# An attention and channel-mix kernel: third and fourth head pair prepared as one tile, five fillers for eight, the last output turned by a DMA, and a new table of order

## The chip, the cores and the metric

The kernel runs on one core of a Trainium2 chip. A core has TensorE (PE: matrix multiplications, its weight loads are shown apart as PEld), VectorE (DVE), ScalarE (ACT), GpSimd (POOL) and SyncE (SP, which here only issues DMAs). Each engine takes its instructions in the order in which they were written, and waits for others by semaphores. The metric is the device time of one execution in microseconds (us), as the median of several runs; one further execution was profiled.

## The reference, cut to what matters

```python
# q, k, v: (4, 8, 768, 64) float32; proj: (64, 6)
q_bits = (q @ proj > 0);  k_bits = (k @ proj > 0)          # 6 bits per token
mask   = q_bucket[..., :, None] == k_bucket[..., None, :]  # bucket = the 6 bits as a number
scores = where(mask, (q @ k.T) / sqrt(64), -1e9)
attn   = softmax(scores);  o = attn @ v
x      = o with heads side by side                          # (4, 768, 512)
x_prev = x one token earlier, 0 for the first
xk = mu_k * x + (1 - mu_k) * x_prev;  xr likewise with mu_r
kk = max(xk @ w_k, 0);  vv = kk * kk @ w_v
out = sigmoid(xr @ w_r) * vv                                # (4, 768, 512) float32
```

It is a hash-masked attention over 4 batches of 8 heads, followed by a channel mix (below: the mix) with weights w_k (512 x 1024), w_v (1024 x 512) and w_r (512 x 512).

## The kernel before, in words

**Pairs.** The 32 heads are worked in 16 pairs, numbered 0 to 15, four pairs to a batch. A pair goes through these steps, each of them an operation of a plan (`add`), with the name that this text uses:

- load: `ldq` brings q and k (float32) into the tile `nat`, `ldv` brings v into `vn`, all issued on SP (L330, L335).
- prepare: q and k are split into two half-precision parts in the tile `nh`: `hi` (L398, DVE) is the rounded value, `lo` (L401, DVE) the rest. Then `tr` (L405, a DMA transpose issued on SP) turns `nh` into the tile `a`, with the head's 64 rows of `hi` over 64 rows of `lo`. For pairs 0 and 1 (`add_prep_turn`, L446) all of this is done by PE transposes (L478, L512) with evacuations on ACT and DVE, since DMAs are slow to arrive at the start; there `hi` is L467, the bits come out of PE as L489 and go into `nh` by L497 (`ex`), and the turned tile is evacuated by L517 (`evt`).
- bits (`bits`, L427, PE): the six projections of q and k, in 16 small matmuls; `bx` (L431, DVE) makes signs of them; four `row` copies (L443, POOL) write the sign rows of q and k of both heads into the tile `a`, so that the product of q and k also tells whether the buckets agree.
- scores (`sc`, L544, PE): 9 steps of 1024 columns per pair, each into a PSUM tile of two banks; `exp` (L548, ACT) takes each step to the tile `pt`. A step needs the sign rows of the heads and halves that its columns touch.
- `oo` (L571, PE): the weighted sum of v, three groups of 12 matmuls for each of the two heads; `rc` (L582, L584, L585) and `ob` (L589) normalise it on DVE. For pairs 0 to 3 a thirteenth matmul (L566) adds a small constant.
- turn: the 128 columns of the pair are turned for the mix, either by six PE transposes (`ot`, L599) and a DVE copy (`xt`, L602), or by a DMA transpose on SP (`otd`, L605). Which pairs go by PE is the tuple `OT_PE` (L40).
- mix inputs: DVE makes the shifted difference and `xk`, `xr` (L612, L630 to L644).

After the fourth pair of a batch its mix follows (`add_moe`, L648): `kp` (L659, PE) with relu on ACT (L663) and squares on DVE (L666), `r` (L679, PE) with a tanh on ACT (L682), `v` (L692, PE), the product `os` on DVE (L699) and the store `st` on SP (L702). The weights of the mix are loaded by `wl` (SP) and cast by `wc` (L304, POOL).

**Order.** The operations are not emitted as they are added. `Plan.schedule` (L123) puts them out in the order of a table, `ORDER` (L17), whose numbers are the places at which the operations were added, and gives each PSUM user a bank from a second table, `BANKS` (L72). So each engine's sequence is fixed by hand, and an instruction that is not ready holds up all that stand behind it on its engine. A PSUM bank that is taken again adds a wait for the operation that read it last.

**Whole or in halves.** `MERGED` (L37) lists the pairs whose q and k are prepared together (`add_prep`, L390): one `hi`, one `lo` over 24 blocks and one transposing DMA. Pairs 2 and 3 are not in it: they have a `hi`, a `lo` and a `tr` for q and another for k, 12 blocks each. `nh` has two buffers, `nat` three, so that `hi` of a pair waits for the transpose of the pair two earlier, and a load for `lo` of the pair three earlier.

**Fillers.** PE starts with 14 matmuls on zeros (L246) and has 8 fillers of two such matmuls each (L251), strewn by `ORDER` among the first steps of the work.

Of the kernel before, what the change touches and what calls it, by code (L numbers as in the profile page):

```python
# [128 lines left out]
def kernel(  # L129
# [34 lines left out]
    MERGED = tuple(range(4, 16))  # L164
    FIRSTS = (0, 1)
    JOINT = ()
    OT_PE = (0, 1, 2, 3, 15)
# [611 lines left out]
```

## Time and profile before

| what | us |
|---|---|
| median of 3 runs (lowest and highest) | 243.16 (242.25 to 243.25) |
| the profiled execution's own time | 242.0 |
| span in that profile, first to last instruction | 240.2 |
| PE busy | 234.1 (97%) |
| ACT busy | 181.9 (76%) |
| DVE busy | 179.8 (75%) |
| POOL busy | 99.7 (41%) |
| granted TensorE clock | 1.00 throughout |

How to read it: the profiled execution ran 1.2 us under the median, and its own time is 1.8 us over its span. Busy shares are averages over stages that differ: attention of the first pairs alone, attention and mix side by side, and the last mix alone. In rows of the timeline, what stands ahead is the start and the duration of a merged piece in us from the start of the span; a merged piece's duration reaches to the end of its last instruction, and neighbours on a pipelined engine overlap by some hundredths.

### The profile page before, as it was taken

The page shows a single profiled execution, that of the slowest core. Times are in us where ns is not written, and L with a number is a line of the kernel's source. Part 1 is how long each engine was busy: PE and PEld are TensorE (multiplying, and loading weights), DVE is VectorE, ACT ScalarE, POOL GpSimd, SP SyncE. Part 2 cuts the span into 40 slices and gives each one's busy share as a digit, 9 for nine tenths or more (in the row PEclk, how much of TensorE's full clock was granted, in tenths as well). Part 3 has the DMA queues.
Part 4 walks back from the last instruction along what each step waited for, and adds up shares of the span by engine and source line. Part 5 has one row for each costly group of instructions (what it writes and reads, how often), then busy time and mean ns, then how long its engine had stood idle before and what let it go on. Part 6 is the DMA issues. An engine that isn't in the chain of part 4 may idle for free.

```text
span 240.2 us, 6251 instructions
## 1 busy us (share of the span) xinstructions
PE 234.1 (97%) x2515; PEld 147.8 (62%) x2532; DVE 179.8 (75%) x388; ACT 181.9 (76%) x242; POOL 99.7 (41%) x148
## 2 busy tenths in 40 slices
PE   8999999999999999999999999999999999999994
PEld 6985776776766565656456656665566564455442
DVE  3488789999998898989868896887167867348232
ACT  2699999999999999889779999677884640256320
POOL 4064979989934899438087302550000000000000
PEclk9999999999999999999999999999999999999999
DMA  6989999999999999988999989401500401210333
GB/s 225 304 222 274 232 242 260 279 197 362 279 253 284 273 213 294 249 302 206 276 163 241 249 177 234 136 0 26 173 0 3 120 3 44 87 46 1 131 135 131
DMA packets 72605, 44.00 MB, mean 183 GB/s; under 512 B 54912, under 2 KB 67584, under 8 KB 72576
## 3 DMA queue, kind: packets, MB, share of 16 engines
q1 hardware_dynamic: 72208, 43.20, 70.9%
q8 instruction: 20, 0.33, 0.6%
q10 hardware_dynamic: 368, 0.39, 0.5%
q14 instruction: 9, 0.07, 0.1%
HBM read 24.12 MB, written 6.29 MB: 127 GB/s over the span
## 4 chain that ended last, share of the span: by engine, by line
PE 92%; ACT 5%; issue 1%; DVE 0%
PE ps_all L544 25%; PE ps_all L692 17%; PE ps_all L659 16%; PE ps_all L571 14%; PE ps_all L679 8%; ACT pt L548 4%; PE ps_all L427 4%; PE ps_all L489 2%; PE ps_all L512 1%; PE ps_all L478 1%; ACT kr L663 1%; PE ps_all L251 1%; PE ps_all L246 1%; PE ps_all L599 1%; PE ps_all L566 1%
## 5 line engine op out<-in xcount | busy, mean ns | idle before, releaser
L548 ACT ACTIVATE pt<-ps_all 128x1024 bf16<-128x1024 f32 x144 | 138.4, 1041 | 10.9 <-PE ps_all L544 10.3
L544 PE MATMUL ps_all<-a 128*128 128x256 f16 (+1 forms) x384 | 79.2, 325 | 0.5 <-ACT pt L548 0.3
L443 POOL COPY a<-bx 6x384 f32<-6x384 f32 x56 | 38.9, 695 | 34.4 <-DVE bx L431 19.6
L544 PEld LDWEIGHTS <-a 128*128 128x128 f16 x384 | 34.0, 98 | 23.5 <-issue 4.6
L659 PE MATMUL ps_all<-xk,wk 128*128 128x384 bf16 x256 | 48.3, 326 | 0.1
L571 PEld LDWEIGHTS <-pt 128*128 128x128 bf16 x1152 | 42.5, 97 | 8.0 <-issue 0.5
L692 PE MATMUL ps_all<-wv,k 128*128 128x512 bf16 (+2 forms) x199 | 45.6, 362 | 0.5
L571 PE MATMUL ps_all<-va,pt 128*128 128x65 bf16 x1152 | 44.8, 193 | 0.0
L663 ACT ACTIVATE kr<-ps_all 128x384 bf16<-128x384 f32 x64 | 29.4, 491 | 16.0 <-PE ps_all L659 14.4
L659 PEld LDWEIGHTS <-wk 128*128 128x128 bf16 x256 | 24.2, 98 | 17.0 <-issue 0.6
L692 PEld LDWEIGHTS <-k 128*128 128x128 bf16 x208 | 19.3, 98 | 18.9 <-issue 0.3
L699 DVE SCALAR_TENSOR_TENSOR os<-rs,ps_all 128x512 f32<-128x512 f32 (+2 forms) x26 | 16.5, 643 | 19.0 <-PE ps_all L692 13.7
L682 ACT ACTIVATE rs<-ps_all 128x512 f32<-128x512 f32 x24 | 14.3, 602 | 20.5 <-PE ps_all L679 14.1
L666 DVE TENSOR_TENSOR k<-kr 128x384 bf16<-128x384 bf16 x64 | 23.2, 389 | 8.3 <-ACT kr L663 8.3
L401 DVE SCALAR_TENSOR_TENSOR nh<-nat,nh 128x1536 f16<-128x1536 f32 (+1 forms) x16 | 27.0, 1694 | 0.2
L679 PE MATMUL ps_all<-wr,xr 128*128 128x512 bf16 x88 | 23.2, 379 | 0.4
L356 POOL TENSOR_TENSOR vt<-vn 128x384 f32<-128x384 f32 x12 | 17.8, 1485 | 12.5 <-DMA vn<-in_v_dram 11.7
L589 DVE TENSOR_TENSOR ob<-ps_all,rc 128x384 bf16<-128x384 f32 x32 | 17.5, 553 | 1.4 <-DMA xt<-ob 0.8
L431 DVE TENSOR_SCALAR bx<-ps_all 128x768 uint16<-128x768 uint16 x14 | 13.4, 956 | 5.3 <-PE ps_all L427 4.7
L398 DVE TENSOR_SCALAR nh<-nat 128x1536 f16<-128x1536 f32 (+1 forms) x16 | 15.8, 985 | 0.3 <-PE ps_all L512 0.2
L679 PEld LDWEIGHTS <-xr 128*128 128x128 bf16 x96 | 9.0, 98 | 9.0
L380 DVE SCALAR_TENSOR_TENSOR va<-ps_all,vn 128x384 bf16<-128x384 f32 x24 | 12.7, 548 | 0.5 <-PE ps_all L375 0.2
(77 smaller groups left out, 188.9 us busy)
## 6 DMA issues: line engine op xcount, KB each, us to landing
vn<-in_v_dram SPq DMA_DIRECT2D x16, 384.0 KB, 5.1
out_dram<-os SPq DMA_DIRECT2D x23, 256.0 KB, 2.3
nat<-in_k_dram SPq DMA_DIRECT2D x15, 384.0 KB, 4.7
nat<-in_q_dram SPq DMA_DIRECT2D x15, 384.0 KB, 5.2
wst<-in_moe_w_k_dram SPq DMA_DIRECT2D x2, 512.0 KB, 7.0
wst<-in_moe_w_r_dram SPq DMA_DIRECT2D x2, 512.0 KB, 5.8
wst<-in_moe_w_v_dram SPq DMA_DIRECT2D x2, 512.0 KB, 4.4
k<-in_moe_w_k_dram SPq DMA_DIRECT2D x1, 512.0 KB, 4.4
```

Source lines behind the costliest of these rows:

```text
L356: e.tensor_tensor(out=vt[:, :, :, 0:E], in0=src[:, :, 0:3, 0:E], in1=src[:, :, 3:6, 0:E], op=ALU.add)
L401: nc.vector.scalar_tensor_tensor(out=nh[:, :, D:P], in0=nat.rearrange("p j (c d) -> p (j c) d", d=D), scalar=QS, in1=nh[:, :, 0:D], op0=AL ...
L443: nc.gpsimd.tensor_copy(side_a[side][n % NAQ][D : D + NB, j, :].bitcast(FP32), bx_t[sx][32 * i : 32 * i + NB, :].bitcast(FP32))
L544: nc.tensor.matmul(ps[:, lo - s * STEP : hi - s * STEP], side_a["k"][sa][:, j, jc * P : (jc + 1) * P], side_a["q"][sa][:, j, q0 : q0 + hi ...
L548: nc.scalar.activation(out=pt_t[sp][:, s * STEP : (s + 1) * STEP], in_=ps_t[plan.slot[nm]], func=AF.Exp, bias=EBIAS, scale=ESC)
L571: nc.tensor.matmul(oo[:, ic * 65 : ic * 65 + 65], pt_t[sp][:, o : o + P], va_t[sa][:, j, jc, 0 : D + 1], start=(not uc and ic == 0 and jc ...
L589: nc.vector.tensor_tensor(out=ob_t[so][:, :, j * D : (j + 1) * D], in0=oo[:, :, 0:D], in1=rc_t[sr][:, 1, :].unsqueeze(2).to_broadcast([P, ...
L659: nc.tensor.matmul(ps[:, 0:HALF], wk_sb[:, d, fc * P : (fc + 1) * P], xk_t[mx[d]][:, h * HALF : (h + 1) * HALF], start=(d == 0), stop=(d = ...
L663: nc.scalar.activation(out=kr_t[sk], in_=sm(nm)[:, 0:HALF], func=AF.Relu, scale=0.5 ** 0.5)
L666: nc.vector.tensor_tensor(out=k2_t[s2][:, h * HALF : (h + 1) * HALF], in0=kr_t[sk], in1=kr_t[sk], op=ALU.mult)
L679: nc.tensor.matmul(sm(nr), xr_t[mx[d]][:, c * P : (c + 1) * P], wr_sb[:, d, :], start=(d == 0), stop=(d == NDC - 1))
L692: nc.tensor.matmul(sm(nv)[:, x0:x1], k2_t[(b * NFC + fc) % NK2][:, c * P : (c + 1) * P], wv_sb[:, fc, x0:x1], start=(fc == 0), stop=(fc == ...
```

## The change

Five edits come together.

1. `MERGED` takes in pairs 2 and 3: for each of them two `hi`, two `lo` and two transposing DMAs of 12 blocks become one of each of 24 blocks.
2. Eight fillers become five; the three that go are those which stood between the scores of pairs 2 and 3.
3. `OT_PE` loses pair 15: its output is turned by a DMA on SP instead of six PE transposes and a DVE copy.
4. `ORDER` has new numbers for all operations behind the head. (The head, up to the first scores, has the same sequence on PE.)
5. `BANKS` is new.

The diff, with the tables cut:

```diff
 ORDER = [
-    0, 16, 2, 3, 4, 21, 5, 6, 7, 20, 8, 9, 10, 11, 37, 41, 33, 26, 1, 29, 28, 36, 30, 32, 40, 69, 72, 71, 70, 74, 73, 25, 43, 27, 31, 79,
...
+    0, 34, 66, 69, 38, 30, 23, 31, 16, 68, 71, 1, 26, 25, 2, 33, 3, 67, 70, 4, 27, 20, 29, 37, 74, 22, 5, 109, 6, 40, 24, 28, 7, 19, 44, 8,
...
 BANKS = [
-    2, 6, 2, 0, 4, 0, 0, 0, 0, 4, 4, 0, 3, 7, 1, 5, 4, 6, 1, 4, 5, 3, 4, 5, 2, 3, 4, 5, 4, 3, 0, 1, 2, 3, 0, 0, 0, 1, 7, 6, 6, 0, 2, 2, 2,
...
+    3, 5, 2, 0, 0, 6, 7, 6, 5, 6, 5, 4, 3, 5, 2, 4, 3, 3, 0, 2, 1, 0, 3, 5, 3, 2, 3, 0, 1, 2, 0, 1, 2, 0, 2, 1, 0, 1, 3, 2, 1, 1, 1, 1, 1,
...
-    MERGED = tuple(range(4, 16))
+    MERGED = tuple(range(2, 16))
...
-    OT_PE = (0, 1, 2, 3, 15)
+    OT_PE = (0, 1, 2, 3)
...
-    for i in range(8):
+    for i in range(5):
         def filler(i=i):
```

Lines of the changed kernel are one less than those of before from the fillers on.

What the tables do to the order is read from the built programs. First, DVE from the sign step of the first pair to the sign step of the third (`nh_61` with `nat_60` is pair 2, `nh_62` with `nat_58` pair 3, `nh_61` with `nat_59` pair 4; `bx_67` is pair 2's signs). Before:

```order
L497 TENSOR_SCALAR nh_61<-ps_all 128x6x6
L398 TENSOR_SCALAR nh_61<-nat_60 128x12x64
L517 COPY a_63<-ps_all 128x768
L398 TENSOR_SCALAR nh_61<-nat_60 128x12x64
L401 SCALAR_TENSOR_TENSOR nh_61<-nat_60,nh_61 128x12x64 x2
L497 TENSOR_SCALAR nh_62<-ps_all 128x12x6
L275 TENSOR_SCALAR mur<-mur 128x4
...
L398 TENSOR_SCALAR nh_62<-nat_58 128x12x64
L401 SCALAR_TENSOR_TENSOR nh_62<-nat_58,nh_62 128x12x64
L431 TENSOR_SCALAR bx_67<-ps_all 128x768
L401 SCALAR_TENSOR_TENSOR nh_62<-nat_58,nh_62 128x12x64
```

And in the changed kernel, the same stretch:

```order
L496 TENSOR_SCALAR nh_61<-ps_all 128x6x6
L516 COPY a_63<-ps_all 128x768
L397 TENSOR_SCALAR nh_61<-nat_60 128x24x64
L400 SCALAR_TENSOR_TENSOR nh_61<-nat_60,nh_61 128x24x64
L274 TENSOR_SCALAR mur<-mur 128x4
L496 TENSOR_SCALAR nh_62<-ps_all 128x12x6
...
L397 TENSOR_SCALAR nh_62<-nat_58 128x24x64
L400 SCALAR_TENSOR_TENSOR nh_62<-nat_58,nh_62 128x24x64
L430 TENSOR_SCALAR bx_67<-ps_all 128x768
L397 TENSOR_SCALAR nh_61<-nat_59 128x24x64
L581 RECIPROCAL rc_89<-ps_all 128x6
L588 TENSOR_TENSOR ob_92<-ps_all,rc_89 128x6x64
```

The first half of pair 2's `hi` no longer stands ahead of the copy L517, `mur` has moved ahead of the sign step of pair 1 (L497 with `nh_62`), and the whole `lo` of pair 3 stands ahead of pair 2's `bx`, where only its first half stood.

Second, SP from the last early load of q to the transposes of pair 3 (`a2_65` is pair 2, `a3_66` pair 3). Before:

```order
L330 DMA nat0_58<-in_q_dram 128x2x384
L405 DMA_TRANSPOSE a2_65<-nh0_61 128x12x128 x2
L330 DMA nat1_59<-in_k_dram 128x2x384
L335 DMA vn2_71<-in_v_dram 128x2x384
L330 DMA nat1_59<-in_q_dram 128x2x384
L273 DMA muk_135<-in_moe_mu_k_dram 128x4x1
L335 DMA vn0_69<-in_v_dram 128x2x384
L405 DMA_TRANSPOSE a3_66<-nh1_62 128x12x128 x2
```

And in the changed kernel:

```order
L329 DMA nat0_58<-in_q_dram 128x2x384
L334 DMA vn2_71<-in_v_dram 128x2x384
L329 DMA nat1_59<-in_k_dram 128x2x384
L404 DMA_TRANSPOSE a2_65<-nh0_61 128x24x128
L329 DMA nat1_59<-in_q_dram 128x2x384
L272 DMA muk_135<-in_moe_mu_k_dram 128x4x1
L334 DMA vn1_70<-in_v_dram 128x2x384
L329 DMA nat2_60<-in_k_dram 128x2x384
L334 DMA vn0_69<-in_v_dram 128x2x384
L404 DMA_TRANSPOSE a3_66<-nh1_62 128x24x128
```

Two loads moved ahead of pair 2's transpose, and one load more stands between the two pairs' transposes.

Third, POOL around the sign rows of pairs 2 and 3 (the `COPY` rows into `a2_65` and `a3_66`; `vt0_72` and `vsu` are sums over v). Before:

```order
L443 COPY a2_65<-bx0_67 6x384 x4
L350 CAST va2_80<-vn2_71 128x12x64
L350 CAST va0_78<-vn0_69 128x12x64
L356 TENSOR_TENSOR vt0_72<-va2_80 128x390
L359 TENSOR_TENSOR vt0_72<-vt0_72 128x2x65
L362 TENSOR_TENSOR vsu0_75<-vt0_72 128x130
L269 MEMSET xt3_97 128x1
L269 MEMSET xt0_94 128x1
L443 COPY a3_66<-bx1_68 6x384 x4
```

And in the changed kernel:

```order
L442 COPY a2_65<-bx0_67 6x384 x2
L268 MEMSET xt0_94 128x1
L442 COPY a2_65<-bx0_67 6x384 x2
L268 MEMSET xt5_99 128x1
L355 TENSOR_TENSOR vt0_72<-va2_80 128x390
L358 TENSOR_TENSOR vt0_72<-vt0_72 128x2x65
L361 TENSOR_TENSOR vsu0_75<-vt0_72 128x130
L349 CAST va0_78<-vn0_69 128x12x64
L355 TENSOR_TENSOR vt0_72<-va0_78 128x390
L442 COPY a3_66<-bx1_68 6x384 x4
```

The cast of pair 2's v moved to before the rows of pair 2, and the first sum of pair 3's v to before the rows of pair 3. By the numbers of `ORDER`, the four rows of pair 3 come as q1, k1, q0, k0 before and as q1, q0, k1, k0 after (letter for side, digit for head).

On PE, between the bits of pair 2 and the first scores of pair 2, there stand before: sc1_7, sc1_4, sc1_5, two groups of oo0_1, two of oo0_0, sc1_0, a group of oo0_0; and after: sc1_7, oo0_1, sc1_3, oo0_1, sc1_0, oo0_0, sc1_4, oo0_0 (sc1_7 is step 7 of pair 1; oo0_1 a group of pair 0, head 1). The last steps on PE are v3_5_256, v3_5_384, v3_5_0 before, and v3_5_384, r3_5, r3_4, v3_4, v3_5_0 after (batch 3, chunk of 128 tokens, first column).

115 rows, old and new, of tables (BANKS, ORDER) are left out of this document.

## The prediction

> **What bounds the kernel now.** I read the page's busy shares and chain first, then the busy time by windows, then the timeline of the first 36 us and of the last 40. The page has the chain that ended last almost wholly on PE:
>
> ```profile
> PE 92%; ACT 5%; issue 1%; DVE 0%
> L548 ACT ACTIVATE pt<-ps_all 128x1024 bf16<-128x1024 f32 x144 | 138.4, 1041 | 10.9 <-PE ps_all L544 10.3
> ```
>
> The windows tell where that holds alone. The cut at 11.6 is the start of the first exp, that at 98 where ACT begins to have gaps:
>
> ```profile
> core 0: us, PE busy (x) PEld busy (x) DVE busy (x) ACT busy (x) POOL busy (x), PEclk, DMA share, GB/s
> 11.60:98.00 86.40, 85.83 (x1181) 58.80 (x1181) 78.92 (x149) 85.43 (x104) 67.31 (x79) 1.00 1.09 261
> 98.00:236.90 138.90, 137.88 (x1250) 80.01 (x1262) 96.06 (x226) 91.23 (x131) 29.03 (x44) 1.00 0.49 131
> 80.00:90.00 10.00, 9.62 (x146) 6.20 (x144) 9.26 (x21) 10.00 (x12) 8.92 (x10) 1.00 1.02 241
> ```
>
> From 11.6 to 98 us two engines are full: PE lacks 0.57 us of 86.40 and ACT 0.97. From 98 to the last matmul PE lacks 1.02 of 138.90, and ACT is busy for 66%. So every us that PE works or waits is a us of the end, except that before 98 ACT can hold PE up. There is almost no idle PE time to win (0.57 + 1.02 = 1.6 us), but any new wait in PE's fixed sequence costs its length.
>
> **What is removed.** Three fillers and six transposes leave PE. Their price is the distance to the next matmul of another line:
>
> ```profile
> 26.95 0.38 PE L251 MATMUL ps_all<-k 128*128 128x256 bf16 x2
> 27.17 0.53 PE L571 MATMUL ps_all<-va,pt 128*128 128x65 bf16 x12
> 201.56 0.50 PE L599 MATMUL ps_all<-idb,ob 128*128 128x128 bf16 x6
> 201.90 1.03 PE L679 MATMUL ps_all<-wr,xr 128*128 128x512 bf16 x4
> ```
>
> A filler is 0.22, so three are 0.66; the transposes are 0.34. Together PE loses **1.0 us** of work. The copy L602 of pair 15 leaves DVE, which is not full there. In its place a DMA turns pair 15:
>
> ```profile
> xt<-ob SPq DMA_TRANSPOSE x11, 4.1
> 202.37 0.55 DVE L602 COPY xt<-ps_all 128x768 bf16<-128x768 bf16 x1
> 208.81 3.41 PE L659 MATMUL ps_all<-xk,wk 128*128 128x384 bf16 x20
> ```
>
> The new order puts the last group of oo15 some 3 us earlier on PE, and the kp of batch 3, which need the turned tile, about 9 us behind it (r2_0, r2_3, a kp of batch 2, eight half chunks of v, r2_1, r2_2). The rc and ob that follow oo15 and the 4.1 us of the DMA run beside these; what DVE does after landing (shift, difference, xk: about 1.8 us) still ends some 2 us before kp. I cost it at nothing; if that cover were gone, a late landing would stop PE by what it is late.
>
> **What the joint preparation costs: pair 2.** These rows are DVE before, and pair 4's joint `hi` and `lo` as the price of one whole:
>
> ```profile
> 11.15 0.20 DVE L497 TENSOR_SCALAR nh<-ps_all 128x36 uint16<-128x36 uint16 x1 [0.95 <-PE ps_all L489]
> 11.27 0.55 DVE L398 TENSOR_SCALAR nh<-nat 128x768 f16<-128x768 f32 x1
> 12.02 0.56 DVE L517 COPY a<-ps_all 128x768 f16<-128x768 f16 x1 [0.21 <-PE ps_all L512]
> 12.50 0.55 DVE L398 TENSOR_SCALAR nh<-nat 128x768 f16<-128x768 f32 x1
> 13.08 1.83 DVE L401 SCALAR_TENSOR_TENSOR nh<-nat,nh 128x768 f16<-128x768 f32 x2
> 15.21 0.23 DVE L497 TENSOR_SCALAR nh<-ps_all 128x72 uint16<-128x72 uint16 x1 [0.30 <-PE ps_all L489]
> 15.36 0.26 DVE L275 TENSOR_SCALAR mur<-mur 128x4 f32<-128x4 f32 x1
> 15.53 0.43 PEld L512 LDWEIGHTS <-nh 128*128 128x128 f16 x6
> 24.39 1.10 DVE L398 TENSOR_SCALAR nh<-nat 128x1536 f16<-128x1536 f32 x1
> 25.52 1.94 DVE L401 SCALAR_TENSOR_TENSOR nh<-nat,nh 128x1536 f16<-128x1536 f32 x1
> ```
>
> Before, half of `hi` ran at 11.27 while DVE waited for L517's input. After, all of it stands behind L517: it starts at 12.50, `lo` at 13.63 and ends at 15.57. `mur` now comes next, so the sign step of pair 1 starts at about 15.75 instead of 15.21, and the transposes that wait for it on PE at 16.07 instead of 15.53. **PE waits 0.55 us** here. Everything behind on PE, and the next exp on ACT, moves by as much.
>
> **Pair 3, and the sign rows of pair 2.** PE then reaches the bits of pair 2. They need its transpose, and these rows price it:
>
> ```profile
> 14.07 3.40 SPq L405 DMA_TRANSPOSE a<-nh  x2
> 22.27 4.29 SPq L405 DMA_TRANSPOSE a<-nh  x2
> 28.16 5.02 SPq L405 DMA_TRANSPOSE a<-nh  x1
> DMA to landing us min/median/max: 3.9/6.9/9.5
> 21.53 0.83 PE L427 MATMUL ps_all<-a,p 128*32 128x512 f16 x16
> 22.49 0.96 DVE L431 TENSOR_SCALAR bx<-ps_all 128x768 uint16<-128x768 uint16 x1 [0.24 <-PE ps_all L427]
> 23.36 0.95 DVE L401 SCALAR_TENSOR_TENSOR nh<-nat,nh 128x768 f16<-128x768 f32 x1
> 19.52 1.26 DVE L517 COPY a<-ps_all 128x768 f16<-128x768 f16 x2 [0.20 <-PE ps_all L512]
> 23.58 4.82 POOL L443 COPY a<-bx 6x384 f32<-6x384 f32 x4 [2.77 <-issue]
> ```
>
> A joint transpose issued at 15.57 lands at 22.5 by the median and at 25.1 by the longest. I take about 7.2, a little over that median because halves are in it, so 22.8. PE comes to the bits at 21.53 + 0.55 + about 0.7 (two groups of oo and sc1_5 now stand ahead, sc1_3 behind), 22.8, so there is no wait, with +2.3 as the far end. But the bits' reader `bx` is late: the last L517 of pair 1, which ended at 20.78, ends at about 21.0 (0.55 later, less 0.3 since its PE transposes now stand one score step further ahead), and the whole `hi` (1.10) and `lo` (1.94) of pair 3 stand ahead, so `bx` starts at 24.05 instead of 22.49. The rows start at 25.1, take 4.82 / 4 = 1.2 each, and the two that the first scores need end at 27.5. PE gets there sooner; its pieces are
>
> ```profile
> 26.68 0.43 PE ps_all L544 x3
> 24.26 0.73 PE ps_all L571 x24
> 31.46 0.77 PE ps_all L427 x16
> ```
>
> that is 0.43 a step, 0.365 a group, 0.77 the bits: 22.8 + 0.77 + 4 x 0.43 + 4 x 0.365 = 26.75. **PE waits 0.85 us** for the rows.
>
> Whether a row takes 1.2 is a choice: the mean of all 56 is 0.695, by which two rows would end at 26.5 and nothing would wait; the slow ones lie beside L401 on DVE, and after the change the rows lie beside pair 4's `hi` and `lo`, so I take 1.2. The Trainium skill ("GPSIMD Engine Reference", section "Specifications") says that GpSimd shares its SBUF interfaces with VectorE and contends with DVE instructions that have two SBUF inputs or run in a 2-port mode; the trace agrees, with 1.2 beside L401 against 0.695 on average.
>
> Next on DVE after `bx` come pair 4's `hi`, one `ob`, `muk`, pair 4's `lo` (1.94) and only then the other `ob` of pair 0, which ends at about 29.75. PE's transposes of pair 0 (`ot0`) are reached at about 29.4: **0.4 us**. The bits of pair 3 then start at about 31.8 instead of 31.39. Since their place has 0.65 us less PE work ahead of it (a filler, and steps moved behind), PE has been idle 0.41 + 0.65 = **1.06 us** more than before up to there. That is less than the three waits' 1.8, because some 0.7 us of short waits before lay in the same stretch.
>
> **Sign rows of pair 3.** Its transpose, issued at 24.0, lands by 31.2 and is in time. `bx` ends at 33.6; the rows then take 4.41 / 4 = 1.1 each:
>
> ```profile
> 33.42 4.41 POOL L443 COPY a<-bx 6x384 f32<-6x384 f32 x4 [1.49 <-issue]
> ```
>
> The first step of pair 3 (sc3_5) needs q1 and k1, which were the first two rows and are now the first and third: 33.7 + 3.3 = 37.0. PE arrives 4.6 after the bits' start (bits, six steps, three groups, rounded up for the thirteenth matmul), at 36.4: **0.6 us**.
>
> **Sum.** -1.0 + 1.06 + 0.6 = +0.7 us against the profiled 242.0, so 242.7. The profiled execution lies 1.16 under the median; against the median 243.16 the forecast is **243.9**, +0.3%. Everything behind pair 3 is costed at nothing: PE and ACT stay full and the sequences there are of the same kind. At the end, the last store (256 columns) is as before, but the store in front of it is now a whole chunk, at worst 0.3.
>
> **Rivals.**
>
> *The waits do not appear (not slower).* If the rows take 0.7 and DVE starts pair 2's whole earlier than I think, the sum is -1.0, so 242.2; with the 1.6 us of old idle time used as well at best 240.6. For it: the waits hang on tenths of DVE's sequence. Against: `hi` can't start before L517, whose input ended a wait of 0.21 already.
>
> *The fillers were free.* ACT is full from 11.6 to 98 (85.43 of 86.40), so PE may only wait where fillers stood, and 0.66 us of the gain is not there: 244.6. For it: ACT starts late as well, since sc0_8 waits behind the same transposes. Against: the page has PE, not ACT, on the chain, and PE has mix work of its own from 57 us on.
>
> *The joint transposes land late (slower).* With 9.5 us each, pair 2's bits start at 25.1 instead of 22.8 and the rows' wait shrinks by 0.45: +1.85 more, 245.8; with pair 4's rows, which now wait on POOL behind a weight cast whose load is issued behind pair 4's transpose, about 1 us more, 246.8. It decides from a landing over 7.2 us. For it: the DMA engines' share is 1.09 there; pair 4's took 8.4. Against: the second half of pair 2, issued behind the first, landed at 19.7, 5.7 after the first issue. The landings of pair 4's transpose and of that half:
>
> ```profile
> L405 SPq DMA_TRANSPOSE a<-nh x1: 5022/5022/5022, 28.2 to 28.2; - x1
> DMA to landing us min/median/max: 8.4/8.4/8.4
> ```
>
> ```profile
> L405 SPq DMA_TRANSPOSE a<-nh x1: 1917/1917/1917, 15.5 to 15.5; - x1
> DMA to landing us min/median/max: 4.2/4.2/4.2
> ```
>
> *The clock falls.* The first fillers run at half rate:
>
> ```profile
> 2.86 0.64 PE ps_all L246 x3
> ```
>
> 0.21 each, against 0.11 each at 26.95. Three us of PE at that rate would cost 1.5 us: 245.4. But no wait that I expect is over 0.85, and PEclk is 1.00 in every window. The Trainium skill ("TensorE: Matmul & The Clock Gate", part 1) has the clock fall only after an idle window of about 3.4 us; no run here shows such a gap.
>
> **How the numbers follow.** About 0.5% (1.2 us) is what a measurement of this kernel can tell from no change. Forecast 0.35, the waits absent 0.28, free fillers 0.15, late landings 0.20, clock 0.02. Under 241.94 lies the better part of the second case: faster 0.18. Over 244.38 lie the late landings and the clock, over half of the free fillers and a little of the forecast: slower 0.38. The rest, 0.44, is within. The range reaches from 241.2 (the second case with half of the old idle time won) to 246.8 (late landings with pair 4). The likeliest case by itself is 243.3 to 244.6.
>
> **What would show it.** In the changed profile: L496 of pair 1 at about 15.75 on DVE and the transposes L511 at 16.07; `bx` of pair 2 at 24.05, with the joint `lo` just ahead; PE idle before the first scores of pair 2, released by POOL L442; bits of pair 3 at 31.8; ACT's first 20 exps about 1 us later than before; kp of batch 3 without a wait. It is wrong if the order behind 40 us has waits of its own on PE, which I priced at nothing, or if PE fills those of the head with work that I took to be fixed.

## The result, and the profile after

| | median, us | lowest to highest | runs |
|---|---|---|---|
| before, on the same chip | 242.7 | 241.81 to 244.39 | 20 |
| after | 243.88 | 242.5 to 246.8 | 20 |

The ratio is 1.0044, with a 95% interval of 1.0027 to 1.0062: slower by 1.1 us, just under what was called tellable. The ratio is taken over the fast runs, which leaves out the three of after that took over 246 us, the profiled one among them.

The number forecast, 243.9, is the number measured, and that is luck in two ways. The forecast stood on a median of three runs, 243.16, which 20 runs put at 242.7: the change forecast was +0.7 us, the change measured +1.1. And most of the waits it was made of are not there, while others are. The runs of after also spread more, 4.3 us against 2.6. The profiled execution took 246.6, at the long end, so its waits are larger than those of a middle run.

The page of after has a new entry on the chain that ended last, and the view of the waits says which instruction it holds:

```profile
PE 79%; DMA 11%; POOL 4%; ACT 3%; DVE 1%; issue 1%; DVEq 0%; POOLq 0%; ACTq 0%
L426 PE MATMUL ps_all<-a,p 128*32 128x512 f16 (+1 forms) x224 | 11.7, 328 | 3.3 <-DMA a<-nh 3.2
```

```profile
engine line waited for: us in total, times, longest us
PE ps_all L426 <- DMA a<-nh: 3.2, 3, 1.6
...
PE ps_all L543 <- POOL a L442: 0.4, 1, 0.4
```

(From the fillers' place on, a line of after has a number one less than in before; in some kernels below two or three less.) Before, DMA had no share of the chain. After it has 11%: the bits (L426) wait for transposed q and k to land, for which nothing waited before. The pieces of the chain and the windows tell where:

```profile
24.59 8.73 DMA a<-nh
...
49.39 8.43 DMA a<-nh
...
75.71 10.28 DMA a<-nh
```

```profile
11.60:98.00 86.40, 82.62 (x1123) 56.36 (x1123) 76.65 (x140) 82.71 (x101) 63.28 (x75) 1.00 1.12 255
98.00:241.00 143.00, 142.27 (x1319) 82.55 (x1317) 98.86 (x232) 94.76 (x136) 34.74 (x47) 1.00 0.54 133
30.00:40.00 10.00, 8.08 (x126) 5.35 (x123) 7.72 (x12) 8.41 (x10) 7.94 (x9) 1.00 1.13 214
80.00:90.00 10.00, 8.78 (x152) 6.32 (x152) 8.76 (x18) 8.90 (x11) 7.71 (x9) 1.00 1.14 255
```

The chain's rows are start, duration and what: the transposes of pairs 3, 6 and 8 are themselves the path. PE (the first number behind the comma) lacks 3.8 us of the first window where it lacked 0.57 before, and 3.1 of that is in the two stretches of 10 us with the landings of pairs 3 and 8; from 98 us on it lacks 0.73. The clock stays at 1.00. The first of these waits on PE, and the queue that leads to it on SP:

```profile
33.37 0.83 PE L426 MATMUL ps_all<-a,p 128*32 128x512 f16 x16 [1.60 <-DMA a<-nh]
```

```profile
16.08 4.40 SPq L404 DMA_TRANSPOSE a<-nh  x1
20.66 0.44 SPq L329 DMA_DIRECT2D nat<-in_q_dram  x1
21.16 0.45 SPq L272 DMA_DIRECT2D muk<-in_moe_mu_k_dram  x1
21.72 0.44 SPq L334 DMA_DIRECT2D vn<-in_v_dram  x1
22.20 0.47 SPq L329 DMA_DIRECT2D nat<-in_k_dram  x1
22.77 0.41 SPq L334 DMA_DIRECT2D vn<-in_v_dram  x1
24.59 6.71 SPq L404 DMA_TRANSPOSE a<-nh  x1
```

The whole `lo` of pair 2 ends later than its first half did, so pair 2's transpose is issued at 16.08 and not from 14.07 on, and holds SP for 4.40. Four loads of 384 KB go out between 20.66 and 23.2, and 1.4 us behind the last comes the transpose of pair 3. It holds SP for 6.71 and lands at 33.32, 8.73 us after its issue; the bits start at 33.36. So from here on the transposes of pairs 4 to 8 are issued later too, because SP is held.

**How profiles are compared below.** The first exp (L547) starts anywhere from 11.3 to 12.9 us in these profiles. So I compare the stretch from the first exp's start to the start of PE's last weight load: 236.30 - 11.60 = 224.70 before, 240.26 - 12.48 = 227.78 after. Three limits of this measure:

- What lies ahead of the first exp is left out. It starts at 11.32 to 12.77 in the seven profiles with the old order (middle 11.98) and at 11.79 to 12.92 in the seven with the new one (middle 12.47). Whether the new order starts later on average is not shown by so few.
- What lies behind the last weight load is left out as well, and there the new order loses: up to the end of the span it takes 3.8 to 4.0 us in all seven profiles with the old order (240.2 - 236.30 = 3.9 before), and 4.2 to 4.3 in five of the seven with the new one (244.5 - 240.26 = 4.2 after; 3.8 and 6.1 in the other two). That is about 0.35 us of the 1.1.
- Five profiles have the old order unchanged up to pair 14 (two of them with three fillers fewer). Their bits of pair 4 start 28.04 to 28.05 us after the first exp, but by the bits of pair 6 two of them are 0.45 and 0.89 late, where nothing was changed. A difference of this size in one profile counts for something only with the wait that it comes from.

### The profile page after: what moved, and what is told of

Its sections match the earlier page's. It is cut to its first block, busy times and chain, and to the rows that moved or that the text cites. A ratio compares the mean times of both kernels' runs of the same rounds, so it can differ in the third digit from the quotient of the medians.

```text
span 244.5 us, 6249 instructions
## 1 busy us (share of the span) xinstructions
PE 235.3 (96%) x2520; PEld 147.9 (60%) x2520; DVE 179.8 (74%) x383; ACT 181.8 (74%) x242; POOL 101.4 (41%) x148
## 4 chain that ended last, share of the span: by engine, by line
PE 79%; DMA 11%; POOL 4%; ACT 3%; DVE 1%; issue 1%; DVEq 0%; POOLq 0%; ACTq 0%
PE ps_all L543 18%; PE ps_all L691 17%; PE ps_all L658 16%; DMA a<-nh 11%; PE ps_all L570 9%; PE ps_all L678 8%; PE ps_all L426 4%; ACT pt L547 3%; POOL a L442 2%; PE ps_all L488 2%; PE ps_all L245 1%; PE ps_all L477 1%; PE ps_all L511 1%; PE ps_all L250 1%; DVE bx L430 1%
## 5 line engine op out<-in xcount | busy, mean ns | idle before, releaser
L547 ACT ACTIVATE pt<-ps_all 128x1024 bf16<-128x1024 f32 x144 | 138.7, 1038 | 17.0 <-PE ps_all L543 16.1
L442 POOL COPY a<-bx 6x384 f32<-6x384 f32 x56 | 43.5, 777 | 45.3 <-DVE bx L430 40.8
L658 PE MATMUL ps_all<-xk,wk 128*128 128x384 bf16 x256 | 49.0, 326 | 0.0
L543 PEld LDWEIGHTS <-a 128*128 128x128 f16 x384 | 33.4, 98 | 23.6 <-issue 4.4
L691 PE MATMUL ps_all<-wv,k 128*128 128x512 bf16 (+2 forms) x208 | 46.2, 363 | 0.0
L665 DVE TENSOR_TENSOR k<-kr 128x384 bf16<-128x384 bf16 x64 | 23.6, 387 | 17.4 <-ACT kr L662 17.2
L400 DVE SCALAR_TENSOR_TENSOR nh<-nat,nh 128x1536 f16<-128x1536 f32 x14 | 25.8, 1845 | 0.2
L678 PE MATMUL ps_all<-wr,xr 128*128 128x512 bf16 x96 | 24.1, 379 | 0.0
L397 DVE TENSOR_SCALAR nh<-nat 128x1536 f16<-128x1536 f32 x14 | 15.4, 1098 | 0.3 <-DMA nat<-in_k_dram 0.3
L426 PE MATMUL ps_all<-a,p 128*32 128x512 f16 (+1 forms) x224 | 11.7, 328 | 3.3 <-DMA a<-nh 3.2
```

Of the source, the lines that this page charges most:

```text
L400: nc.vector.scalar_tensor_tensor(out=nh[:, :, D:P], in0=nat.rearrange("p j (c d) -> p (j c) d", d=D), scalar=QS, in1=nh[:, :, 0:D], op0=AL ...
L426: nc.tensor.matmul(ps[32 * i : 32 * i + 32, lo:hi], w_, side_a[side][m % NAQ][:, j, lo:hi], start=(x == 0), stop=(x == len(mats) - 1))
L442: nc.gpsimd.tensor_copy(side_a[side][n % NAQ][D : D + NB, j, :].bitcast(FP32), bx_t[sx][32 * i : 32 * i + NB, :].bitcast(FP32))
L543: nc.tensor.matmul(ps[:, lo - s * STEP : hi - s * STEP], side_a["k"][sa][:, j, jc * P : (jc + 1) * P], side_a["q"][sa][:, j, q0 : q0 + hi ...
L547: nc.scalar.activation(out=pt_t[sp][:, s * STEP : (s + 1) * STEP], in_=ps_t[plan.slot[nm]], func=AF.Exp, bias=EBIAS, scale=ESC)
L658: nc.tensor.matmul(ps[:, 0:HALF], wk_sb[:, d, fc * P : (fc + 1) * P], xk_t[mx[d]][:, h * HALF : (h + 1) * HALF], start=(d == 0), stop=(d = ...
```

## The experiments

Theory 1, from the profile after: **late landings** are the loss. Theory 2: **the new order** has waits of its own at fixed places. Theory 3 (the rival on record): **the fillers were free**.

### The changed kernel once more

```diff
 (no edit)
```

> The changed kernel once more, for a second profile. Late landings (the joint transposes land as PE reaches the bits, and how late differs from execution to execution): 0.2 to 0.7% over before, and in the profile the bits L426 wait for the DMA a<-nh, but at other pairs or by other lengths than the 1.6 us at pair 3 and 1.6 us at pair 8 of the first profile; sum 1 to 5 us. Head sequence (DVE's whole steps delay PE, as the prediction had it): the same three waits each time, 0.55 at L511, 0.85 at the first scores of pair 2, 0.4 at L598, and none at the bits.

Measured 243.55 (242.28 to 247.12), before 242.82: ratio 1.003 (1.000 to 1.006). Its profile, with a stretch of 226.65, has both kinds of wait:

```profile
PE ps_all L426 <- DMA a<-nh: 1.5, 2, 0.8
...
PE ps_all L543 <- POOL a L442: 0.5, 1, 0.5
...
PE ps_all L511 <- DVE nh L496: 0.3, 1, 0.3
```

Which landings are late differs from execution to execution (pairs 3, 6 and 8 in the one, 3 and 9 here); pair 3 is late in both, with 8.73 and 8.2 us. Both executions are long ones, 246.6 and 246.08. Of three profiles below of the new order with its own bits, after_loads_behind, after_mended and after_mended_loads, which took 242.1 to 244.1, one has such a wait, at pair 3 (after_mended).

### Pairs 2 and 3 in halves again, and the other way round

```diff
 # after_split23: the changed kernel; the halves' instructions stand where the wholes stood
-    MERGED = tuple(range(2, 16))
+    MERGED = tuple(range(4, 16))
 # before_merged23: the kernel before; the whole stands where the later half stood
-    MERGED = tuple(range(4, 16))
+    MERGED = tuple(range(2, 16))
```

> The changed kernel with pairs 2 and 3 in halves again, the halves at the places of the wholes (hi q, hi k, lo q, lo k, then both transposes). Late landings: the transposes' first halves go out some 1 us earlier and land in 4 to 6 us, so the wait at the bits of pair 3 (1.6 us in the first profile) is gone, and the time falls by 1 to 1.8 us, to the level of before or 0.2% under it. Head sequence: DVE does the same work ahead of pair 2's bx as with wholes, so the time stays within 0.2% of the changed kernel.

> The kernel before with pairs 2 and 3 as wholes, each whole at the place of its later half; everything else as before. Late landings: pair 3's transpose goes out at 24.4 as one and lands 7 to 9 us later, at 31.4 to 33.4, where PE is at its bits at 31.4: 0.5 to 1.5 us slower than before, all of it in a wait at these bits. Head sequence: pair 1's sign step is late by 0.5 us and little else, since pair 3's lo stands behind bx here: 0.2 to 0.5 us slower, with no wait at the bits.

Halves in the changed kernel: 243.43, ratio to before 1.001 (0.9984 to 1.0035), against 1.003 for the changed kernel on the same chip: too near to tell. Halves placed where the wholes stand are issued no sooner: the first at 24.52, and the second lands at 33.6.

Wholes in the kernel before: 244.84, ratio 1.0073 (1.0044 to 1.0102), the only clear loss by one part so far, and not by the bits, so neither theory had it. PE and POOL there:

```profile
48.26 1.03 PE L542 MATMUL ps_all<-a 128*128 128x256 f16 x5 [1.31 <-POOL a L441]
```

```profile
44.17 1.28 POOL L354 TENSOR_TENSOR vt<-vn 128x384 f32<-128x384 f32 x1 [2.13 <-DMA vn<-in_v_dram]
45.52 2.69 POOL L441 COPY a<-bx 6x384 f32<-6x384 f32 x2
```

```profile
31.61 6.17 SPq L403 DMA_TRANSPOSE a<-nh  x1
...
38.97 0.47 SPq L333 DMA_DIRECT2D vn<-in_v_dram  x1
```

Read from below: pair 4's transpose holds SP until 37.78; the load of v for pair 4 stands behind it and goes out at 38.97 (34.36 before); the sum over v on POOL waits 2.13 for that; the sign rows of pair 4 stand behind the sum; PE waits 1.31 for them. One held queue stops POOL, and POOL stops PE.

### Bits that don't need the new landing

```diff
-    ..., w_, side_a[side][m % NAQ][:, j, lo:hi], ...
+    ..., w_, side_a[side][(m - 1) % NAQ][:, j, lo:hi], ...
```

The bits of a pair are taken from the tile of the pair before it, so this kernel leaves the right signs out. Its sign rows still wait for the pair's own landing.

> The changed kernel, its bits taken from the pair before, whose turned tile landed long ago: this leaves out the right signs, and the wait of the bits for their own pair's transpose at all pairs. The sign rows still wait for the landing, which hides up to 2 us of lateness behind bits and bx. Late landings: no idle time of PE before L426 for a<-nh, 1 to 2.5 us faster than the changed kernel, 0.2 to 0.8% under before, and a narrower spread. Head sequence: no change over 0.2%, since the bits are not late in it.

Measured 243.75, ratio 1.0035 (1.0005 to 1.0065): no gain. Theory 1 alone falls. In this profile pair 3's transpose landed in 6.5 us (with the same loads ahead of it), PE had no wait for a landing anywhere, and the stretch was still 225.50, 0.8 over before. What is left in it are three waits: at the first transposes of pair 1 (the bits of pair 2 start 11.49 after the first exp, against 11.01 in profiles without this wait, so 0.48), 0.32 idle ahead of sc3_5, and 0.87 idle at sc9_2, for a sign row of POOL. That speaks for theory 2, with a reservation: the first wait is missing in the profile after, and the third is 0.37, 0.51 and 0.87 in three profiles of this order and missing in after_loads_behind below. They are not of one size each time.

### Each small part alone

```diff
 # before_5fillers
-        for i in range(8):   # fillers
+        for i in range(5):
 # before_otd15
-    OT_PE = (0, 1, 2, 3, 15)
+    OT_PE = (0, 1, 2, 3)
 # before_5f_otd15: both
```

> The kernel before without three of its fillers (the one that stands in scores 2_7 to 3_5, the one in 3_5 to 2_8 and one more of the steady ones), nothing else moved. If TensorE sets the end there (the prediction's first step), the time falls by 3 x 0.22 = 0.66 us, to 242.2 beside 242.8. If the fillers stand where TensorE waits for ScalarE or for rows anyway (the rival of the free fillers), the time stays at 242.8 and a wait of 0.2 us each appears in their places.

> The kernel before with the output of pair 15 turned by a DMA transpose, in the place where TensorE turned it, nothing else moved. Prediction: 0.34 us less (one group of six transposes on TensorE), landing in 2.7 us before the projection's batch needs it: 242.5 beside 242.8. Rival: the projection's last batch waits for the landing and the time rises by up to 2 us.

> The kernel before with both of these parts, three fillers fewer and pair 15 turned by DMA, and without the joint transposes and the new order. If both parts are worth what the prediction's first steps gave, 0.66 + 0.34 = 1.0 us: 241.8 beside 242.8, and this beats both kernels. If the fillers were free, 242.5.

Three fillers fewer: 242.92, ratio 1.0007 (0.9979 to 1.0036). The profile is plainer than the ratio: from the first exp on, the bits of pair 3 start at 19.78 (19.79 before), those of pair 8 at 70.52 (70.52), the stretch is 224.71 (224.70). **The 0.66 us of fillers were free** in the old order, theory 3 holds: a gain of 0.66 would be 0.27%, outside the interval. PE now waits where a filler stood, for the exps of ACT:

```profile
37.77 0.33 PE L565 MATMUL ps_all<-vsu,tiny 128*128 128x390 bf16 x1 [0.24 <-ACT pt L547]
```

Pair 15 by DMA, in the old place: 243.72, ratio 1.0034 (1.0014 to 1.0054), so it costs 0.9 where 0.34 was to be won; both together cost 1.0047 (1.0025 to 1.0068). The reason on SP, DVE and PE:

```profile
190.03 11.67 SPq L604 DMA_TRANSPOSE xt<-ob  x2
201.76 5.25 SPq L701 DMA_DIRECT2D out_dram<-os  x4
```

```profile
204.19 0.69 DVE L698 SCALAR_TENSOR_TENSOR os<-rs,ps_all 128x512 f32<-128x512 f32 x1 [2.74 <-DMA out_dram<-os]
```

```profile
204.93 1.24 PE L691 MATMUL ps_all<-wv,k 128*128 128x512 bf16 x5 [1.17 <-DVE os L698]
```

Two transposes are merged in the first row, of pairs 14 and 15. The second waits on SP for the last half of pair 15's output, and a store stands behind it until 201.76 (190.16 before); DVE waits 2.74 for the buffer that this store empties, and PE for DVE. To test that:

```diff
 SP: otd14,
-    otd15, st1_3,
+    st1_3, otd15,
     st2_0, st2_1
```

> The kernel before with pair 15 turned by a DMA transpose that stands on SP behind the store that it held up (1_3), not ahead of it. Theory 'SP in order': in the run with the transpose ahead, it waited for the second half of pair 15's output until 200.5 with that store behind it, VectorE's output step of store 2_0 waited 2.74 for the buffer, TensorE 1.2 to 1.3 for that; with the store ahead this goes and only the removed 0.34 us of TensorE is left: 242.5 beside 242.8. Theory 'landing': the wait is for the transposed output itself, and the time stays at 243.7.

Measured 242.45, before 242.66, ratio 0.9991 (0.9969 to 1.0013). The wait is gone:

```profile
190.43 1.26 SPq L604 DMA_TRANSPOSE xt<-ob  x1
191.74 0.57 SPq L701 DMA_DIRECT2D out_dram<-os  x1
200.90 1.21 SPq L604 DMA_TRANSPOSE xt<-ob  x1
```

From the bits of pair 15 to the last weight load it takes 0.27 less than before (80.94 against 81.21), near the 0.34 that left PE; the total is too near to 1 to be called faster. The changed kernel's own order has no such wait.

### The loads moved out of the transposes' way

```diff
 SP: tr2, ldq4q, muk,
-    ldv4, ldq5k, ldv3, tr3, ldq5q, ldq6q, tr4, wl1
+    ldv3, tr3, ldq5k, ldq5q, ldv4, tr4, ldq6q, wl1
```

> The changed kernel with two loads (v of pair 4, k of pair 5) moved on SP's queue from just ahead of the transposing DMA of pair 3 to behind it, and the load of q of pair 6 from ahead of that of pair 4 to behind it. Theory 'late landings': the loads that are still running when the joint transposes are issued make them land late; without them pair 3's lands in 6.5 us or less and not 8.2 to 8.7, bits of pair 3 don't wait, the times over 245 become rare, and the median falls by 0.3 to 0.6 us, to 243.0 beside 243.5 of the changed kernel. Theory 'order': the loss lies in waits that the new order brings at fixed places (0.5 at the transposes of pair 1, 0.5 at the first scores of pair 3, about 1 at scores 9_2): the median stays at 243.4 to 243.8 whatever the landings do.

Measured 243.56 (242.12 to 245.5), ratio 1.0046 (1.0016 to 1.0075). Pair 3's transpose holds SP for 3.8 and not 6.7, and lands in 5.5:

```profile
L403 SPq DMA_TRANSPOSE a<-nh x1: 3814/3814/3814, 25.3 to 25.3; - x1
DMA to landing us min/median/max: 5.5/5.5/5.5
```

No bits wait for a landing any more, and the stretch is 224.63, that of before (224.70). But the median hardly moved: the 0.3 to 0.6 us expected of theory 1 did not come. The times over 245 are 3 of 12, against 5 of 12 and 5 of 20 in the two measurements of the changed kernel, which is nothing to go by. This profile's span is 1.6 over that of before (241.8 against 240.2), and 1.32 of it is its later first exp, 0.35 its end. What makes the median of all twelve runs slower than before, by more than the 0.35 of the end, stays open.

### The order's own waits mended, without and with the loads

```diff
 DVE:  lo2,
-      mur,
       ex1k0, hi1q0, evt1k1,
+      mur,
 POOL: row3q1,
-      row3q0, row3k1,
+      row3k1, row3q0,
       row3k0
 POOL:
-      wc6,
       row9k0, row9q0,
+      wc6,
       wc8
```

> The changed kernel with three places of its new order put as the kernel before had them: on VectorE the cast of mu_r stands behind the sign step L496 of pair 1 and not ahead of it; on POOL the row q1 and then k1 of pair 3 come first; on POOL a cast of the sixth MoE weight stands behind the first two rows of pair 9 and not ahead. Theory 'order': the waits of 0.5 at the transposes of pair 1, 0.5 at scores 3_5 and 0.4 to 1.0 at scores 9_2 go, the time falls by 1 to 1.3 us beside the changed kernel's 243.5, to 242.4. Theory 'the waits are cover': TensorE waits later for the same exponentials or landings, and the time stays within 0.4 of 243.5.

> The same with the three loads behind the joint transposes as well. Theory 'order and landings': 242.2 to 242.4, with no run above 245, and it beats the kernel before by 0.5 us. If only the waits of the order count, as after_mended; if neither, 243.5.

| | median, us | ratio to before, 95% | first exp | bits of pair 3, after it | stretch |
|---|---|---|---|---|---|
| mended | 244.07 | 1.0062 (1.0041 to 1.0083) | 12.07 | 20.50 | 225.52 |
| mended, loads behind | 243.02 | 1.0006 (0.9985 to 1.0027) | 11.79 | 19.22 | 224.25 |
| not mended, loads behind | 243.56 | 1.0046 (1.0016 to 1.0075) | 12.92 | 19.71 | 224.63 |

Mended alone is no faster than the changed kernel; with the loads moved as well it takes 1.05 us less, and is level with the kernel before. Two profiles of PE and SP show why, first mended alone:

```profile
32.57 0.72 PE L425 MATMUL ps_all<-a,p 128*32 128x512 f16 x12 [1.20 <-DMA a<-nh]
```

```profile
23.81 6.72 SPq L403 DMA_TRANSPOSE a<-nh  x1
```

then with the loads behind:

```profile
31.02 0.83 PE L425 MATMUL ps_all<-a,p 128*32 128x512 f16 x16
```

```profile
23.53 3.61 SPq L403 DMA_TRANSPOSE a<-nh  x1
```

The mending makes PE come to the bits of pair 3 sooner by 0.5. With the loads ahead, though, the landing is 20.4 after the first exp (32.5 - 12.07), as in the changed kernel (33.32 - 12.48 = 20.8), so PE waits longer at the bits. With the loads behind nothing waits there, and the 0.5 stays. The two other mendings show no gain of their own. At sc3_5 PE idles as long as before, and it is an exp of ACT that ends this, as it did in the profile after (first row) and does in that of after_mended (second row):

```profile
38.66 0.59 PE L543 MATMUL ps_all<-a 128*128 128x256 f16 x3 [0.32 <-ACT pt L547]
...
37.87 0.59 PE L542 MATMUL ps_all<-a 128*128 128x256 f16 x3 [0.32 <-ACT pt L546]
```

The wait at sc9_2 is gone in both mended profiles, but it is not there with the loads behind alone either.

### The mirror: the loads put in the way in the kernel before

```diff
 SP: tr2, tr2, ldq4k, ldv2, ldq4q, muk,
-    ldv3, tr3, tr3, ldq5q, ldq5k, tr4, ldq6q, ldq6k, ldv4
+    ldv4, ldq5k, ldv3, tr3, tr3, ldq5q, tr4, ldq6q, ldq6k
```

> The kernel before with the same two loads (v of pair 4, k of pair 5) put ahead of the transposing DMAs of pair 3 on SP, where the changed kernel has them; halves, fillers and order as before. Theory 'loads in flight set the landing': the halves of pair 3, issued 22 to 24 and landed in 4.7 to 5.4 us, now land 1.5 to 3 us later, the 1.5 to 2.0 us between landing and bits of pair 3 go, and the time rises to 243.2 to 244.0 beside 242.7. Theory 'only one joint transpose is slow under loads': the halves land as before, and the time stays within 0.3 of 242.7.

Measured 244.08, before 242.93, ratio 1.0053 (1.0018 to 1.0087): **two loads moved on a queue cost as much as the whole change.** The halves of pair 3 now hold SP for 7.98 instead of 4.29:

```profile
22.65 7.98 SPq L404 DMA_TRANSPOSE a<-nh  x2
```

```profile
L404 SPq DMA_TRANSPOSE a<-nh x2: 3585/3944/4302, 22.7 to 27.0; - x2
DMA to landing us min/median/max: 5.6/7.2/8.7
```

```profile
32.73 0.83 PE L426 MATMUL ps_all<-a,p 128*32 128x512 f16 x14 [0.57 <-DMA a<-nh]
```

The first half takes 8.7 to land and not 6.0; the second is issued at 27.05 instead of 24.34, with a first exp that is 0.38 later, and lands at 32.7. The bits do their first two matmuls and then wait. The landings of pairs 8 and 9 are late here too (bits 0.04 us behind each), and the stretch grows by 1.7 us.

## Why the prediction was right or wrong, point by point

The total was right by luck: about half of the waits it was added up from were the wrong ones, and 0.46 us of the forecast came from the median of three runs that it stood on. Two small slips in its working change nothing: 27.5 - 26.75 is a wait of 0.75 and not 0.85 for the rows of pair 2, and the lower end of the range, 242.2 less half of 1.6, is 241.4 and not 241.2.

- **Fillers, -0.66: wrong.** The step that failed is "every us that PE works or waits is a us of the end" before 98 us. The prediction named the exception, that ACT can hold PE up there, and then did not use it in the sum. The window that it was read from had ACT as full as PE, and ACT decided: the stretch without three fillers is 224.71 against 224.70. The rival that had a chance of 0.15 was right on this mechanism, if not on its 244.6.
- **Transposes of pair 15, -0.34, and its landing at nothing: right** for the changed kernel (0.27 where it was measured alone, no wait at kp of batch 3). But the cover named was PE work, and what decides in the old place is a store behind the transpose on SP: 0.9 us.
- **L511 waits 0.55: right in size.** 0.48, as the bits of pair 2 show it, in three of the five profiles that have this order on DVE. The profile after has hardly any of it: L496 starts at 16.09 there, 0.88 later than before, and the whole kernel's start is 0.88 later. Of the cause I had named `hi`, `lo` and `mur`; it is `mur` that varies:

```profile
15.97 0.16 DVE L274 TENSOR_SCALAR mur<-mur 128x4 f32<-128x4 f32 x1
16.09 0.23 DVE L496 TENSOR_SCALAR nh<-ps_all 128x72 uint16<-128x72 uint16 x1
```

in the profile after, and in that of the changed kernel once more:

```profile
15.66 0.79 DVE L274 TENSOR_SCALAR mur<-mur 128x4 f32<-128x4 f32 x1
16.36 0.22 DVE L496 TENSOR_SCALAR nh<-ps_all 128x72 uint16<-128x72 uint16 x1
16.64 0.51 PE L511 MATMUL ps_all<-idh,nh 128*128 128x128 f16 x6 [0.27 <-DVE nh L496]
```

- **Pair 2's landing in time: right** (22.2, 1.25 us ahead of the bits). **0.85 for its sign rows: wrong.** `bx` came at 24.49, 23.6 with the 0.88 taken off, but the first two rows took 1.66 together and not 2.4. **0.4 at `ot0`: wrong**, no wait there.
- **"Its transpose, issued at 24.0, lands by 31.2 and is in time": wrong, and the dearest step.** It was issued at 24.59 and landed in 8.73 us, and in 8.2 and 8.7 in two more profiles; PE idles 0.84 to 1.60 ahead of the bits there. This is the rival of late landings with its point of decision (over 7.2 us), but at pair 3 and not at pair 2 where I had priced it. I took the median of all landings. The rows that told better were on SP: what is issued just ahead, which the joint `lo` pushes towards pair 3's transpose.
- **0.6 at sc3_5: wrong in its cause.** PE idles there (0.32, shown above), but for an exp of ACT, and as long with the rows in the old order. So the late row is not a term of the sum.
- **Behind pair 3 at nothing: wrong for pairs 4 to 9.** Their bits came 1.2 to 3.1 us behind the landings before, and 0.04 to 2.3 after. In the profile after PE idles 0.38 for it at pair 6 and 1.22 at pair 8. From the bits of pair 10 to the last weight load nothing differs any more: it takes 133.06 or 133.07 in all seven profiles of the new order.
- **The end, "at worst 0.3" and not in the sum: about 0.35.** The stores behind the last weight load take that much longer in five of seven profiles.

As measured, in stretches: the new order without a wait at pair 1 or at a landing is 0.45 us shorter than before (224.25 against 224.70, the turn's 0.3 in it); the wait at pair 1 adds 0.4 where pair 3 lands in time (224.63 against 224.25); a late landing of pair 3 adds 1.3 to 1.7, with that wait or without it, since the earlier wait shortens the later one (its bits start 20.50, 20.62 and 20.89 after the first exp in after_mended, after_again and after, against 19.22 in after_mended_loads); and the end, outside the stretch, adds 0.35. That comes to 1.2 to 1.6 for an execution in which pair 3 is late and 0.3 for one in which it is not; the 1.1 measured lies between. In the two long executions later pairs add more. With the loads behind and the order mended the kernel is level with before (1.0006), while mending alone left 1.0062: that is shown. How much of the 1.1 each part has in a middle run is not. Landings behind the same queue differ from execution to execution (6.5 to 8.7 at pair 3) together with those of the loads ahead of them, as the table at the end shows; why the loads differ stays open, so the 4.3 us of spread are not explained by an experiment of their own.

No kernel here beats the one before by more than its interval; the nearest is pair 15 by DMA with its store ahead (0.9991).

## What to carry to other kernels

When a change merges transfers, or delays one, write down the whole queue from there on, with what each issue holds and what is still in flight, and price the next landing from the rows that have the same transfers just ahead of them. A median over all landings does not do. Before counting removed work as a gain, ask in each window whether a second engine is as full; and remember that a wait mended ahead of a late transfer only moves to the transfer.

## What the runs showed of the hardware

- **A transposing DMA issued close behind loads is slow, and slow to issue.** The same joint transpose of 24 blocks landed in 5.5 us behind three loads (one of them small), and in 8.2 to 8.7 us behind five in three profiles, 6.5 in a fourth; it held SP for 3.6 to 3.8 us in the one case, for 6.2 to 6.7 (4.5 in that fourth) in the other. The count of loads is not what decides: in before_merged23 it landed in 6.0 us behind five, issued 4.0 us after the last of them. What goes with the landing is that of the last load ahead of it, in us from the span's start:

  | profile | last load issued | and landed | transpose of pair 3 issued | and landed | behind the load |
  |---|---|---|---|---|---|
  | after | 22.77 | 30.7 | 24.59 | 33.3 | 2.6 |
  | after_again | 22.48 | 30.2 | 24.55 | 32.8 | 2.6 |
  | after_mended | 22.31 | 29.9 | 23.81 | 32.5 | 2.6 |
  | after_bits_prev | 22.22 | 28.7 | 24.84 | 31.3 | 2.6 |
  | before_merged23 | 22.21 | 27.2 | 26.21 | 32.2 | 5.0 |
  | after_loads_behind | 22.06 | 26.2 | 25.27 | 30.8 | 4.6 |
  | after_mended_loads | 20.89 | 24.9 | 23.53 | 29.0 | 4.1 |

  Where the load lands 3.8 us or more after the transpose's issue, the transpose lands 2.6 us behind it; where it lands within 1.4 us, the transpose takes 5.5 to 6.0 us from its issue. Whether it waits for the loads or shares the DMA engines with them is not shown. The Trainium skill ("DMA: Bandwidth & Descriptors", section "Two DMAs through the same engine are not ordered") says that within a queue of one engine descriptors start in order; a transpose that is slower for what was issued ahead of it agrees with that. The Trainium skill's page "Advanced Engine Details and Errata", section "X-Bar Transpose (TRN2)", expects 350 to 400 GB/s of such transposes; for 24 blocks of 128 x 128 in half precision, 786 KB, that would be 2.0 to 2.2 us, an estimate from that page. No landing here came near it: 5.4 is the shortest of any joint transpose in these profiles, start-up included.
- **A small DVE instruction can take five times its time.** The cast of `mur` over 128x4 took 0.16, 0.26 and 0.79 us in the three profiles quoted here and in the prediction.
- **The start varies by more than the change is worth.** The first exp began at 11.3 to 12.8 us in seven profiles of the old order and at 11.8 to 12.9 in seven of the new, with the same first loads issued in all 14; why is not shown. Comparing spans of single profiles would have misled. Comparing from the first exp on agreed within 0.02 us up to the bits of pair 4 where nothing had changed, and no longer so behind them.
